# A state-space convolution beside a memory attention: one load moved to the head of the second half, and the projections dealt out in another way

## The chip, the cores and the metric

The kernel runs on one core of a Trainium2 chip. The time is device microseconds of one execution; of the kernel before there are three, 894.51, 900.52 and 901.75 us, median 900.52. A further execution was taken with the hardware profiler. Its trace gives every instruction of the engines: TensorE (PE, with its weight loads as PEld), VectorE (DVE), ScalarE (ACT), GpSimd (POOL) and SyncE (SP), which issues most of the DMAs.

## The reference, cut to what matters

The input is `u`, 2048 rows of 448 columns. Two branches are mixed by a gate: `g * a + (1 - g) * b`, with `g = sigmoid(sum(u * gate_w))`.

```
# a: a long convolution per channel d; its kernel K sums 256 decaying rotations
P = exp((A * dt)[:, :, None] * pos)            # [448, 256, 2048], complex
K = 2 * einsum("dn,dnl->dl", C, P).real
y = irfft(rfft(K, 4096) * rfft(u, 4096))[:2048] + u * D_skip
# b: 16 heads of 28, 4 segments of 512 rows, a running memory M, z
p = softmax(q k^T * scale + mask);  a_dot = p v
a_mem = (phi(q) M) / (phi(q) z + 1e-6)
o = sig(beta) * a_mem + (1 - sig(beta)) * a_dot
M += phi(k)^T v;  z += sum(phi(k));  out = o @ wo
```

All is float32. The projections `x @ wq`, `x @ wk`, `x @ wv` are done in split precision, as three products of high and low parts.

## The kernel before, in words

**First half** (`first_half`, line 310). It builds `K`. Channels are taken 16 at a time: `J` runs over 28 blocks, and each block has two passes `n = 2J, 2J+1` of 8 channels. Four passes make a group, numbered `g = n // 4`, from 0 to 13. One factor of a rotation is an exponential (`EY`, `EX`), the other a sine and a cosine (`cs`), and ACT needs another table for Exp than for Sin. So all six exponentials of a group (two blocks, three each, `blk` 0 to 2) are made together, by `decays(g)` (line 427), and the four passes follow. Each exponential takes its argument from a small matmul pair into a PSUM tile `arg`, of which there are two. In the kernel before, `exponents` (line 341) issues that pair and `decay` (line 348) the exponential, and the pair for the next slot is issued ahead of the exponential of this one. The first pair of a group is issued before `sums(n - 1)` of the pass before (line 463), and the eight matmuls of `turns(4 * g)`, the angles of the next pass, come in slot 5, ahead of its exponential (line 435). `turns` uses the same two `arg` tiles.

A pass `n` does, in the order of the program: `turns(n + 1)` on PE, `trig(n)` (three ACT instructions), some of the projections (`feed.spend`), `product(n)` (four DVE instructions into `X` and `Y`), `sums(n - 1)` (64 small matmuls). PE keeps the order of the program; in this half (`k.strict`) so do ACT and DVE.

**Feed** (class at line 472). The projections of the other branch and the first transform of `u` are written as a generator of small steps, each of which tells its cost in us. `spend(us)` adds credit (at most 4.0 in hand) and takes steps until the credit is used. It stops at a step of negative cost, whose result must first be read. It also stops at the mark "pe": two finished projections then hold two of the three PSUM tiles `m` until the next `decay` calls `feed.exps`, which issues their exponentials and copies on ACT (`e`, `hi`, four instructions) while the Exp table is loaded. While feed is held or done, a step of the transform of `u` (`ut`, `gs`) is taken instead. A pass gives 2.0 (line 458), a slot of `decays` 1.1 (line 441). With `k.exps` set (slots 2 to 5), copies of the feed go to DVE instead of ACT.

**Second half** (`second_half`, line 1256). It opens with `transform_k` (line 547), whose PSUM tiles are copied by ACT (line 567) and DVE and stored to `GK`; then 16 units of attention run (`maxima`, `weigh`, `values`), with the convolution (`convolve`, line 574) dealt between them. Here a planner with its own model of time orders the instructions of ACT, DVE, POOL and SP; PE keeps the order of the program. `load_wo` (line 984) is called after the second unit. It loads `wo` and three constants on SP's queue. One of them is the selecting matrix `c_sel` (32 x 512), which goes to a tile `selin` and is copied by ACT into `k.sel`; `spread` (line 1124) uses it to bring reciprocals of denominators to all rows, for the first time at 608 us. `selin` lies in the room of the tile `am`.

Of the kernel before, what the change touches and what calls it, by code (L numbers as in the profile page):

```python
# [12 lines left out]
F32 = mybir.dt.float32  # L13
# [3 lines left out]
AF = mybir.ActivationFunctionType  # L17
# [10 lines left out]
SEG = 512  # L28
# [281 lines left out]
def first_half(nc, k, gy, feed):  # L310
# [3 lines left out]
    NJ = 28  # L314
    act, v = k.act, nc.vector
    lt, EY, EX, kps, arg, cs, XY = {}, {}, {}, {}, {}, {}, {}
    exps = []

    def load_decay(J, queue=nc.sync.dma_start):
        lt[J] = k.lhs[J % 5]  # L320
# [12 lines left out]
    def load(J):  # L333
        if J < NJ:
            load_decay(J)
            load_phase(J)

    def rows(nt):
        return slice(64 * nt, 64 * nt + 64), {"tile_position": (64 * nt, 0)}

    def exponents(J, blk):

        exps.append(k.ps("arg"))
        for nt in range(2):
            r, kw = rows(nt)
            k.mm(exps[-1][:, nt], lt[J][r, 2], k.ce[r, blk], start=True, stop=True, **kw)

    def decay(J, blk):
        pt = exps.pop(0)
        if blk < 2:  # L350
            out = EY[J, blk] = gy.tile([128, 2, 512], F32, tag="EY", name="EY", bufs=6)
        else:
            out = EX[J] = gy.tile([128, 2, 512], F32, tag="EX", name="EX", bufs=2)
        feed.exps()
        act(out, pt, AF.Exp, scale=-1.0)
        if blk == 2 and J > 1:
            scale(J)

    def scale(J):
        o = EX[J]  # L360
        if True:
            cab = k.cab[:, :, 16 * J : 16 * J + 16].unsqueeze(3).broadcast_to([128, 2, 16, 32])
            o = o.rearrange("p t (d c) -> p t d c", c=32)
            nc.gpsimd.tensor_tensor(o, o, cab, ALU.mult)  # L364

    def turns(n):

        J, c = divmod(n, 2)
        arg[n] = pt = k.ps("arg")
        for nt in range(2):  # L370
            r, kw = rows(nt)
            k.mm(pt[:, nt], lt[J][r, c], k.ct[r, 0], start=True, stop=False, **kw)
        for i in range(2):
            for nt in range(2):
                r, kw = rows(nt)
                k.mm(pt[:, nt], k.one[r], k.mag[r, i : i + 1].broadcast_to([64, 512]), start=False, stop=False, **kw)
        for nt in range(2):
            r, kw = rows(nt)
            k.mm(pt[:, nt], lt[J][r, c], k.ct[r, 1], start=False, stop=True, **kw)

    def trig(n):

        pt = arg.pop(n)
        cs[n] = t = gw.tile([128, 2, 2, 2, 256], F32, tag="cs", name="cs", bufs=2)
        pv = pt.rearrange("p t (w c) -> p t w c", w=2)
        act(t[:, 1].rearrange("p w t c -> p t w c"), pv, AF.Sin, scale=TWO_PI)
        act(t[:, 0].rearrange("p w t c -> p t w c"), pv, AF.Abs)
        fl = t[:, 0].rearrange("p w t c -> p (w t c)")
        act(fl, fl, AF.Sin, bias=k.bhp, scale=-TWO_PI)

    def product(n):
        J, c = divmod(n, 2)
        t = cs.pop(n)
        X = gw.tile([128, 2, 2, 256], F32, tag="X", name="X", bufs=2)
        Y = gw.tile([128, 2, 16, 64], F32, tag="Y", name="Y", bufs=2)
        XY[n] = X, Y
        ex = EX[J][:, :, 256 * c : 256 * c + 256].unsqueeze(1).broadcast_to([128, 2, 2, 256])
        v.tensor_tensor(X, ex, t[:, :, 0], ALU.mult)  # L398
        ey = EY.pop((J, c)).rearrange("p t (d c) -> p (t d) c", c=64)
        y = t[:, :, 1].rearrange("p r t (d c) -> p r (t d) c", c=32)  # L400
        lo = ey[:, :, :32].unsqueeze(1).broadcast_to([128, 2, 16, 32])
        v.tensor_tensor(Y[:, :, :, :32], lo, y[:, :, :, ::-1], ALU.mult)  # L402
        v.tensor_tensor(Y[:, 0, :, 32:], ey[:, :, 32:], y[:, 0], ALU.mult)  # L403
        v.scalar_tensor_tensor(Y[:, 1, :, 32:], ey[:, :, 32:], -1.0, y[:, 1], ALU.mult, ALU.mult)  # L404

    def sums(n):
        g, h = divmod(n, 4)
        X, Y = XY.pop(n)
        if h == 0:
            kps[g] = k.ps("k")  # L410
        k.turn_over(kps[g][:, 2 * h : 2 * h + 2], 0)
        for q in range(2):
            for i, (nt, r) in enumerate(((0, 0), (0, 1), (1, 0), (1, 1))):
                for j in range(4):
                    d = 4 * q + j
                    k.mm(
                        kps[g][32 * j : 32 * j + 32, 2 * h + q],
                        X[:, r, nt, 32 * d : 32 * d + 32],
                        Y[:, r, 8 * nt + d],
                        start=(i == 0),  # L420
                        stop=(i == 3),
                        tile_position=(0, 32 * j),
                    )
        if h == 3:
            v.tensor_copy(k.kb[:, :, 8 * g : 8 * g + 8].rearrange("p b q -> p q b"), kps.pop(g))

    def decays(g):
        slots = [(J, blk) for J in (2 * g, 2 * g + 1) for blk in range(3)]
        if g == 0:
            exponents(*slots[0])  # L430
        for i, (J, blk) in enumerate(slots):
            if i < 5:
                exponents(*slots[i + 1])
            elif g > 0:
                turns(4 * g)
            decay(J, blk)
            if g > 0 and i == 4:
                sums(4 * g - 1)
            if g > 0:
                k.exps = i >= 2  # L440
                feed.spend(1.1)
                k.exps = False

    room = []
    yield load_decay, load_phase, functools.partial(decays, 0), room
    gw = room[0]
    scale(0)
    scale(1)
    turns(0)
    for n in range(2 * NJ):  # L450
        if n < 4:
            load(n + 2)
        elif n % 2 == 0:
            load(n // 2 + 4)
        if n % 4 < 3:
            turns(n + 1)
        trig(n)
        feed.spend(2.0)
        product(n)
        if n == 2 * NJ - 1:  # L460
            feed.fill(2)
        if n % 4 == 3 and n + 1 < 2 * NJ:
            exponents((n + 1) // 2, 0)
        if n % 4 > 0:
            sums(n - 1)
        if n % 4 == 3 and n + 1 < 2 * NJ:
            decays(n // 4 + 1)
    feed.fill(4)
    sums(2 * NJ - 1)

# [506 lines left out]
def attend(nc, k, ap):  # L977
# [2 lines left out]
    wo = ap.tile([128, 4, D], F32, name="wo")  # L980
    k.den = ap.tile([128, 128], F32, name="den")
    k.sel = ap.tile([32, 4, 128], F32R, name="sel")

    def load_wo():
        nc.gpsimd.memset(wo, 0.0)
        for j in range(4):
            k.ldma(
                wo[32 * j : 32 * j + 28], k.wo.rearrange("(g j e) c -> j e g c", j=4, e=28)[j]
            )
        k.ldma(k.den, k.c_den)  # L990
        t = ap.tile([128, 4, SEG], F32, tag="am", name="selin", bufs=1)[:32, 0]
        k.ldma(t, k.c_sel.rearrange("p g c -> p (g c)"))
        nc.scalar.activation(k.sel.rearrange("p g c -> p (g c)"), t, AF.Copy)
        k.ldma(k.dbc, k.D_skip.unsqueeze(0).broadcast_to([128, D]))

    Q, K, W, Vs, pvss = {}, {}, {}, {}, {}
# [130 lines left out]
    am = {}  # L1127
# [128 lines left out]
def second_half(nc, k, ap, tp, fp, fin, lp):  # L1256
# [7 lines left out]

    nothing = iter(())
    attend(nc, k, ap)
    k.load(0)
    k.load_rest(0)
# [116 lines left out]
def gated_mix(ctx, tc, k):  # L1385
# [168 lines left out]
    with ExitStack() as st:  # L1554
# [25 lines left out]
        with ExitStack() as s2:  # L1580
            early, prm = pool(s2, "early"), pool(s2, "prm", "right")
            feed = Feed(work(project(nc, k, pp, prm, tu)), tu)
            half = first_half(nc, k, gy, feed)
            load_decay, load_phase, decays, room = next(half)
            params = prepare_params(nc, k, prm, early, gp)
            n = next(params)
            k.ct = gp.tile([128, 2, 512], BF16, name="ct")
            constants()
            while n is not None:
                if n == "decays":  # L1590
                    for J in range(2):
                        load_decay(J, k.pdma)
                    nc.sync.dma_start(k.ct, k.c_ct)
                    decays()
                elif n == "phases":
                    load_phase(0)
                    k.held_by.append(load_phase(1).ins)
                else:
                    feed.until(feed.count + n)
                n = next(params, None)  # L1600
# [69 lines left out]
```

## Time and profile before

| what | value |
|---|---|
| three timed executions | 894.51, 900.52, 901.75 us |
| the profiled execution | 905.99 us, its span 904.2 us |
| mean clock granted to PE over the span | 0.91 |
| first half: the last `sums` end at | 454.8 us |
| Exp and Sin table loads from 115.89 us on | 24, two in each of 12 groups |
| load of `selin`: issue, copy on ACT | 540.00 us, 546.74 us |

A row of the timeline gives the start, the length, the engine, the line, the operation, and the tiles written and read; in square brackets stands how long the engine was idle before, and what ended that. Where a line is that of a helper (1395 for ACT, 1430 for PE), the tile's name tells the instruction. `ps_arg<-ce` are arguments of exponentials, `ps_arg<-ct` and `ps_arg<-mag` are `turns`, `ps_k` are `sums`, `ps_m` are the projections.

### The profile page before, as it was taken

The numbers are of one execution on the slowest core, as the hardware profiler recorded it, in microseconds if no ns is written. First come the engines' busy times: TensorE is split into PE (matmuls) and PEld (weight loads), VectorE is DVE, ScalarE is ACT, GpSimd is POOL, SyncE is SP. The second block draws the span as 40 slices with busy tenths as digits, with TensorE's granted clock in tenths as the row PEclk, the third lists the DMA queues.
The fourth block names the chain that finished last, engine by engine and source line by source line (L and its number), as shares of the span: only waits on it lengthen the run. The fifth ranks groups of instructions, "written<-read, shape, count | busy, mean of one in ns | idle before, by whom it ended". The sixth has DMA issues, their size and how long they took to land.

```text
span 904.2 us, 19002 instructions
## 1 busy us (share of the span) xinstructions
PE 767.8 (85%) x7508; PEld 413.7 (46%) x7517; DVE 600.0 (66%) x1158; ACT 537.1 (59%) x640; POOL 191.0 (21%) x273
## 2 busy tenths in 40 slices
PE   1676997899887999879787997999998999888997
PEld 1353654564454565446443443444444444334433
DVE  7985569766479757687857454556465656665564
ACT  4875689888789788888812344545354534342320
POOL 5222211011110011100100211232323232333210
PEclk9996999999898999989968597999999999888799
DMA  9258844223434324220377765678577575456773
GB/s 234 82 143 287 251 142 133 80 79 107 120 123 127 101 97 150 94 83 14 140 248 270 248 178 149 227 234 279 171 232 253 174 236 179 150 192 226 203 237 100
DMA packets 93408, 153.15 MB, mean 169 GB/s; under 512 B 21544, under 2 KB 58040, under 8 KB 93320
## 3 DMA queue, kind: packets, MB, share of 16 engines
q1 hardware_dynamic: 82104, 136.13, 47.6%
q10 hardware_dynamic: 8032, 10.26, 3.2%
q0 software_dynamic: 3184, 5.56, 2.3%
q8 instruction: 59, 0.97, 0.5%
q14 instruction: 29, 0.24, 0.1%
HBM read 90.91 MB, written 60.63 MB: 168 GB/s over the span
## 4 chain that ended last, share of the span: by engine, by line
PE 56%; DVE 16%; ACT 12%; DMA 8%; issue 5%; SPq 1%; POOL 1%; DVEq 0%; ACTq 0%; POOLq 0%
PE ps_m L1430 18%; PE ps_a L1430 18%; PE ps_pv L1430 8%; PE ps_arg L1430 6%; ACT cs L1395 5%; PE ps_k L1430 4%; DVE jk L1048 4%; DVE Y L402 3%; PE ps_m L1433 2%; DVE X L398 2%; DVE Y L403 1%; DMA RD<-rs 1%; DVE pr L611 1%; ACT hi L1395 1%; ACT L1395 1%
## 5 line engine op out<-in xcount | busy, mean ns | idle before, releaser
L1048 DVE CUSTOM_DVE_ANT_0 jk<-ps_a,mk 128x512 f32<-128x512 f32 (+3 forms) x256 | 125.0, 488 | 55.3 <-PE ps_a L1430 48.2
L1081 ACT ACTIVATE PT<-ps_a 128x1024 f32<-128x1024 f32 (+1 forms) x96 | 84.6, 882 | 119.4 <-PE ps_a L1430 110.1
L364 POOL TENSOR_TENSOR EX<-EX,cab 128x1024 f32<-128x1024 f32 x28 | 54.0, 1931 | 318.3 <-ACT EX L1395 274.2
L1395 ACT ACTIVATE cs<-ps_arg 128x1024 f32<-128x1024 f32 x111 | 107.3, 1020 | 9.7 <-PE ps_arg L1430 8.5
L1430 PE MATMUL ps_a<-qu,ku 32*128 32x512 f32 (+3 forms) x768 | 93.7, 366 | 8.5 <-ACT PT L1081 6.8
L1430 PE MATMUL ps_k<-Y,X 128*32 128x64 f32 x3584 | 67.2, 231 | 30.6 <-DVE Y L403 30.2
L1086 POOL TENSOR_SCALAR_AFFINE_SELECT PT<-PT 128x256 f32<-128x256 f32 x128 | 52.2, 421 | 182.6 <-ACT PT L1081 173.6
L398 DVE TENSOR_TENSOR X<-EX,cs 128x1024 f32<-128x1024 f32 x56 | 69.7, 1245 | 23.2 <-ACT cs L1395 23.1
L1430 PEld LDWEIGHTS ps_k<-Y,X 128*32 128x32 f32 x3584 | 57.5, 117 | 54.5 <-DVE Y L403 44.7
L1430 PE MATMUL ps_m<-xh,w 112*128 112x512 f32 x192 | 76.2, 440 | 1.7 <-ACT gs L1395 1.0
L1430 PEld LDWEIGHTS ps_a<-qu,ku 32*128 32x128 f32 x768 | 65.5, 203 | 16.9 <-ACT PT L1081 7.3
L402 DVE TENSOR_TENSOR Y<-EY,cs 128x1024 f32<-128x1024 f32 x56 | 70.0, 1250 | 0.0
L1430 PE MATMUL ps_arg<-ce,lh 64*128 64x512 bf16 x168 | 40.8, 443 | 30.6 <-ACT EY L1395 20.0
L1395 ACT ACTIVATE cs<-cs,bhp 128x1024 f32<-128x1024 f32 x56 | 64.4, 1151 | 1.8
L1430 PEld LDWEIGHTS <-lh 64*128 64x128 bf16 x392 | 22.5, 96 | 81.3 <-issue 69.1
L1395 ACT ACTIVATE EY<-ps_arg 128x1024 f32<-128x1024 f32 x52 | 52.1, 1040 | 9.2 <-PE ps_arg L1430 9.1
L1430 PE MATMUL ps_a<-ku,qu 32*128 32x512 f32 (+3 forms) x256 | 48.0, 415 | 9.8 <-DVE mx L1048 8.6
L1430 PEld LDWEIGHTS ps_a<-ku,qu 32*128 32x128 f32 x256 | 23.4, 199 | 57.6 <-issue 26.6
L1430 PEld LDWEIGHTS ps_m<-xh,w 112*128 112x128 f32 x192 | 38.1, 198 | 23.6 <-issue 9.4
L404 DVE SCALAR_TENSOR_TENSOR Y<-EY,cs 128x512 f32<-128x512 f32 x56 | 40.5, 725 | 11.7 <-ACT cs L1395 11.0
L1430 PE MATMUL ps_arg<-ct,lh 64*128 64x512 bf16 x224 | 45.3, 390 | 0.8 <-ACT cs L1395 0.8
L1430 PE MATMUL ps_pv<-PT,V 128*32 128x128 f32 (+3 forms) x512 | 45.0, 499 | 0.0
(229 smaller groups left out, 1462.0 us busy)
## 6 DMA issues: line engine op xcount, KB each, us to landing
w<-WD SPq DMA_DIRECT2D x24, 448.0 KB, 3.9
qu<-QD SPq DMA_DIRECT2D x32, 256.0 KB, 4.2
ku<-KD SPq DMA_DIRECT2D x32, 256.0 KB, 4.4
GU<-gs SPq DMA_DIRECT2D x32, 224.0 KB, 2.6
GK<-gs SPq DMA_DIRECT2D x8, 896.0 KB, 3.7
gk<-GK SPq DMA_DIRECT2D x32, 224.0 KB, 5.4
gu<-GU SPq DMA_DIRECT2D x32, 224.0 KB, 2.5
BB<-bs ACTq DMA_DIRECT2D x16, 448.0 KB, 4.8
```

The costliest lines, as they stand in the source:

```text
L364: nc.gpsimd.tensor_tensor(o, o, cab, ALU.mult)
L398: v.tensor_tensor(X, ex, t[:, :, 0], ALU.mult)
L402: v.tensor_tensor(Y[:, :, :, :32], lo, y[:, :, :, ::-1], ALU.mult)
L403: v.tensor_tensor(Y[:, 0, :, 32:], ey[:, :, 32:], y[:, 0], ALU.mult)
L404: v.scalar_tensor_tensor(Y[:, 1, :, 32:], ey[:, :, 32:], -1.0, y[:, 1], ALU.mult, ALU.mult)
L611: nc.vector.tensor_tensor(pr[c], pt, ks.pop(c), ALU.mult)
L1048: v.tensor_tensor_reduce(junk[:, :n], pt[:, x, o : o + n], k.mk[:, SEG - n :], 1.0, -3e38, ALU.add, ALU.max, mx[:, 3 - t, h : h + 1],)
L1081: nc.scalar.activation(PT[b, hp], pt[:, :, :n], AF.Exp, scale=SCALE)
L1086: nc.gpsimd.affine_select(sl, sl, [[0, 2], [1, 128]], ALU.is_ge, 0.0, base=0, channel_multiplier=-1)
L1395: x = op(*args, **kw)
L1430: tc.keep_in_program_order(nc.tensor.matmul(*args, **kw))
L1433: tc.keep_in_program_order(nc.tensor.transpose(*args))
```

## The change

It has three parts. `exponents` goes, and `decay` makes its argument in its own slot, right before its exponential; the first pair of a group no longer goes ahead of `sums`, and `turns(4 * g)` is issued after the last slot. The credit of a pass becomes 2.8 and that of a slot 1.4. The load of `c_sel` goes from `load_wo`, on SP's queue, to the head of the second half, on POOL's, with its copy on ACT behind it.

```diff
-    def exponents(J, blk):
-
-        exps.append(k.ps("arg"))
+    def decay(J, blk):
+
+        pt = k.ps("arg")
         for nt in range(2):
             r, kw = rows(nt)
-            k.mm(exps[-1][:, nt], lt[J][r, 2], k.ce[r, blk], start=True, stop=True, **kw)
-
-    def decay(J, blk):
-        pt = exps.pop(0)
+            k.mm(pt[:, nt], lt[J][r, 2], k.ce[r, blk], start=True, stop=True, **kw)
...
     def decays(g):
-        slots = [(J, blk) for J in (2 * g, 2 * g + 1) for blk in range(3)]
-        if g == 0:
-            exponents(*slots[0])
-        for i, (J, blk) in enumerate(slots):
-            if i < 5:
-                exponents(*slots[i + 1])
-            elif g > 0:
-                turns(4 * g)
-            decay(J, blk)
-            if g > 0 and i == 4:
-                sums(4 * g - 1)
-            if g > 0:
-                k.exps = i >= 2
-                feed.spend(1.1)
-                k.exps = False
+        for J in (2 * g, 2 * g + 1):
+            for blk in range(3):
+                decay(J, blk)
+                if g > 0 and J % 2 and blk == 1:
+                    sums(4 * g - 1)
+                if g > 0:
+                    k.exps = 3 * (J % 2) + blk >= 2
+                    feed.spend(1.4)
+                    k.exps = False
...
-        feed.spend(2.0)
+        feed.spend(2.8)
         product(n)
         if n == 2 * NJ - 1:
             feed.fill(2)
-        if n % 4 == 3 and n + 1 < 2 * NJ:
-            exponents((n + 1) // 2, 0)
         if n % 4 > 0:
             sums(n - 1)
         if n % 4 == 3 and n + 1 < 2 * NJ:
             decays(n // 4 + 1)
+            turns(n + 1)
...
     k.sel = ap.tile([32, 4, 128], F32R, name="sel")
+    selin = ap.tile([128, 4, SEG], F32, tag="am", name="selin", bufs=1)[:32, 0]
+    k.pdma(selin, k.c_sel.rearrange("p g c -> p (g c)"))
+    nc.scalar.activation(k.sel.rearrange("p g c -> p (g c)"), selin, AF.Copy)
 
     def load_wo():
...
         k.ldma(k.den, k.c_den)
-        t = ap.tile([128, 4, SEG], F32, tag="am", name="selin", bufs=1)[:32, 0]
-        k.ldma(t, k.c_sel.rearrange("p g c -> p (g c)"))
-        nc.scalar.activation(k.sel.rearrange("p g c -> p (g c)"), t, AF.Copy)
```

More of the change, by code (lines that the diff above doesn't have):

```diff
@@ L316, in first_half @@
     lt, EY, EX, kps, arg, cs, XY = {}, {}, {}, {}, {}, {}, {}
-    exps = []
     def load_decay(J, queue=nc.sync.dma_start):
```

## The prediction

> **What bounds the kernel now.** I read the page first, for the shares and the chain that ended last.
>
> ```profile
> span 904.2 us, 19002 instructions
> PE 767.8 (85%) x7508; PEld 413.7 (46%) x7517; DVE 600.0 (66%) x1158; ACT 537.1 (59%) x640; POOL 191.0 (21%) x273
> PE 56%; DVE 16%; ACT 12%; DMA 8%; issue 5%; SPq 1%; POOL 1%; DVEq 0%; ACTq 0%; POOLq 0%
> ```
>
> The chain is mostly TensorE, but the change touches the first half (to 455 us) and one load of the second, so each is read by itself. ScalarE changes its table twice in each group of the first half: at the head of `decays` (Exp) and at the head of the four passes behind it (Sin). Those 24 loads cut it into stretches. Here are rows of the view of engine busy time by stretch, first for the decays of groups 2 to 13 (columns: stretch, its length, busy time of PE, PEld, DVE, ACT, POOL, then PE's granted clock), then for the passes.
>
> ```profile
> 144.51:155.10 10.59, 7.53 (x140) 4.63 (x144) 10.16 (x16) 10.05 (x13) 1.91 (x1) 0.84 0.56 167
> 283.02:294.50 11.48, 8.42 (x138) 5.34 (x142) 10.66 (x17) 10.12 (x14) 1.91 (x1) 0.72 0.60 181
> 396.58:407.91 11.33, 8.37 (x150) 5.07 (x142) 10.53 (x16) 10.12 (x14) 1.91 (x1) 0.70 0.34 125
> sum 138.84, PE 116.46 PEld 72.22 DVE 89.08 ACT 111.89 POOL 22.99; mean PE 9.70 PEld 6.02 DVE 7.42 ACT 9.32 POOL 1.92
> ```
>
> ```profile
> 183.82:202.09 18.27, 18.23 (x284) 12.33 (x280) 13.04 (x18) 14.41 (x16) 1.92 (x1) 0.95 0.15 51
> 294.50:313.71 19.21, 18.71 (x298) 11.30 (x290) 14.52 (x19) 14.41 (x16) 1.91 (x1) 0.99 0.33 102
> 326.41:341.33 14.92, 14.92 (x199) 9.95 (x195) 11.84 (x15) 14.42 (x15) 1.92 (x1) 1.00 0.24 81
> 407.91:425.49 17.58, 17.57 (x256) 11.88 (x248) 14.79 (x21) 14.95 (x16) 1.91 (x1) 1.00 0.05 17
> 434.20:449.80 15.60, 12.01 (x235) 7.15 (x232) 13.37 (x17) 14.73 (x17) 2.44 (x2) 0.89 0.34 115
> sum 195.07, PE 171.26 PEld 103.71 DVE 157.41 ACT 174.99 POOL 23.51; mean PE 14.27 PEld 8.64 DVE 13.12 ACT 14.58 POOL 1.96
> ```
>
> In decays ACT is busy 9.32 of 11.57 us on average: ACT sets their length, and PE waits, at a lowered clock. In four passes PE is busy 95% or more and sets the length (the first four rows: mean 17.5). The other eight, of which the last row is one, share (195.07 - 69.98) / 8 = 15.6 us each, whatever projections they carry: ACT and DVE set those. Projections dealt into such a pass are free, up to a point.
>
> Why PE waits in decays is shown by the waits of PE (115.89 to 449.8 us) and the timeline of ACT and PE in group 12.
>
> ```profile
> PE ps_arg L1430 <- ACT EY L1395: 13.7, 7, 2.9
> PE ps_arg L1430 <- ACT EX L1395: 5.3, 6, 1.5
> 396.58 1.28 ACT L1395 ACT_TABLE_LOAD   x1
> 397.87 0.60 ACT L1395 ACTIVATE e<-ps_m 128x512 f32<-128x512 f32 x1
> 399.89 1.05 ACT L1395 ACTIVATE EY<-ps_arg 128x1024 f32<-128x1024 f32 x1
> 396.34 1.10 PE L1430 MATMUL ps_k<-Y,X 128*32 128x64 f32 x64 [1.41 <-DVE Y L403]
> 397.37 0.39 PE L1430 MATMUL ps_arg<-ce,lh 64*128 64x512 bf16 x2
> 397.69 0.65 PE L1433 MATMUL ps_m<-ident,xin 128*112 128x128 f32 x4
> 400.99 0.61 PE L1430 MATMUL ps_arg<-ce,lh 64*128 64x512 bf16 x2 [2.64 <-ACT EY L1395]
> ```
>
> A held pair of projections puts four readings of PSUM ahead of the first exponential (from 397.87 to 399.89). PE, an argument ahead, finds both banks full and stands 2.64 us. Such waits sum to 19.0 us.
>
> **The change part by part.**
>
> *Dealing.* I followed the credits of `feed` step by step, before and after, and priced the steps by the timeline of PE, start to start: from 413.73 to 416.46 there are twelve projection matmuls, so six take 1.36, and three of the slightly longer ones (512 columns for 450) 0.78. The others are 0.91 (`ut`), 1.06 (`macc`, up to the `turns` at 409.15), 0.58 (`ph`), 1.09 (`pkT`, up to the `turns` at 412.76) and 0.65 above (`xin`).
>
> ```profile
> 436.34 0.91 PE L1430 MATMUL ps_m<-ut,s1u 64*128 64x448 f32 x2
> 408.09 1.12 PE L1430 MATMUL ps_m<-ph,macc 128*128 128x512 f32 x2
> 410.12 0.66 PE L1433 MATMUL ps_m<-ident,ph 128*128 128x128 f32 x4
> 410.70 0.39 PE L1430 MATMUL ps_arg<-ct,lh 64*128 64x512 bf16 x2
> 411.67 1.16 PE L1430 MATMUL ps_m<-v,pkT 128*128 128x128 f32 x8
> 413.73 0.47 PE L1430 MATMUL ps_m<-wvh,xh 112*128 112x450 f32 x1
> ...
> 416.46 1.10 PE L1430 MATMUL ps_k<-Y,X 128*32 128x64 f32 x64
> ```
>
> Either way the same 172 us are dealt. Passes of groups 1 to 13 carry, in us: before 9.4, 4.1, 7.4, 7.0, 3.6, 3.5, 3.5, 9.2, 8.0, 6.3, 4.4, 9.3, 3.6; after 11.1, 3.5, 8.8, 10.0, 5.2, 3.8, 9.2, 10.0, 5.2, 3.8, 9.3, 2.7, 0. Decays: before 10.5, 7.9, 4.1, 7.9, 7.4, 7.3, 7.3, 4.2, 6.8, 7.5, 7.5, 4.2, 6.4; after 11.3, 7.9, 4.3, 8.2, 7.3, 7.9, 4.2, 8.2, 7.3, 7.9, 4.2, 7.3, 0. So after, everything is spent in pass 50 of 0 to 55. The last group's 10.0 us, free today (its pass is a 15.6), move forward.
>
> The four PE-set passes carry 7.0, 9.2, 8.0, 9.3: mean 8.4, which leaves 9.1 of their 17.5 as the rest. After, five carry 8.8 or more (47.3 together): 5 x 9.1 + 47.3 = 92.8. Seven light ones at 15.6 make 109.4. Sum 202.2 against 195.07: **+7.1**. Group 1 gets 2.5 more, under loads of weights that hold it anyway: between 0 and +2.5, I take +1, since its feed is the largest of all.
>
> *Arguments in their own slot.* PE no longer runs an argument ahead; ACT's exponential waits for its own matmuls, and queued behind it on ACT are the other exponentials, the table load and the sines that DVE needs. Decays are then PE's: 0.8 us from the table load to the first argument (396.58 to 397.37), six arguments at 0.32 (397.37 to 397.69), one `sums` at 1.03 (396.34 to 397.37), the projections of slots 0 to 4, and one exponential, 1.02: 4.8 + projections. Slot 5 holds 1.09, 1.09, 1.36, 1.56, 0.58, 0.58, 1.36, 1.56, 0.58, 0.58, 0.91 in groups 2 to 12, so slots 0 to 4 hold 74.7 - 11.3 = 63.4 in these eleven, and 11 x 4.8 + 63.4 = 116.2. Three groups (3, 7, 11) begin with transposes that need banks the held pair frees late; today's three such (10.59, 11.48, 11.33) average 11.1 against 8.3 by the formula: +8.4. The last group, without projections, is ACT's, some 7.7. Sum 132.3 against 138.84: **-6.5** at full clock. Of it PE has 63.4 + 11 x 2.95 (arguments and `sums`) = 96 us on the path, and the twelve decays ran at a mean clock of 0.89 (the three shown and nine of 0.75 to 1.00). Between 0.89 (96 / 0.89 - 96 = +11.9, so +5.4 in all) and 1 (-6.5) I take 0.945 (+5.6), since the 19 us of waits that lowered it partly go: **-0.9**.
>
> *`turns(4g)` behind the last slot.* It takes 0.97 (410.70 to 411.67). It is done slot 5's feed + 0.97 after the last argument; ACT needs 1.02 + 1.28 for exponential and table load. Only a slot of over 1.33 makes ACT wait, by 0.23 at most: nothing in the sum, hidden by the table load; at half clock it would be about 1.8 a group.
>
> *The selecting matrix.* Today its load stands behind `wo`, and its copy on ACT ahead of exponentials PE waits for. Timeline, SP's and ACT's queues and PE:
>
> ```profile
> 535.34 3.40 SPq L1446 DMA_DIRECT2D wo<-in_B_wo  x4
> 540.00 0.33 SPq L1446 DMA_DIRECT2D selin<-in_c_sel  x1
> 542.22 0.41 ACTq L625 DMA_DIRECT2D BB<-bs  x1
> 546.74 0.63 ACT L993 ACTIVATE sel<-selin 32x512 fp32r<-32x512 f32 x1 [9.34 <-DMA selin<-in_c_sel]
> 547.28 1.00 ACT L1081 ACTIVATE PT<-ps_a 128x1024 f32<-128x1024 f32 x1
> 548.33 1.01 PE L1430 MATMUL ps_a<-qu,ku 32*128 32x384 f32 x4 [6.80 <-ACT PT L1081]
> ```
>
> Without it, next late is ACT's own issue of `BB`, done at 542.63: the exponential moves from 547.28 to 542.63. Gain between that 4.65 and the whole 9.34; I take **-4.7**, the nearer row, as the loads of `wo` that delay `BB` stay. SP loses one issue of 0.33 there. Added at the head: an issue on POOL, a transfer, a copy of 0.63 on ACT.
>
> ```profile
> 454.84 1.59 POOL L985 MEMSET wo<- 128x1792 f32 x1 [6.10 <-PE ps_k L1430]
> 459.39 0.92 ACT L567 ACTIVATE gs<-ps_a 128x896 f32<-128x896 f32 x1 [9.19 <-PE ps_a L1430]
> qu<-mn POOLq DMA_DIRECT2D x32, 8.0 KB, 3.5
> ```
>
> Room comes free at about 454.84. With the 3.5 us of POOL's small loads it lands at some 458.9 with its issue, in the 9.19 us that ACT stands idle: 0. With the 6.7 that it took from 540.00 to 546.74, it lands at 462.1, and the first `gs`, if queued behind the copy, starts 3.3 us late with PE's banks behind it. I take 0. POOL's own next work can wait (its next DMA starts 30 us later).
>
> [...]
>
> *Sum:* +7.1 + 1 - 0.9 - 4.7 = **+2.5** on the profiled execution (905.99, its span 904.2 and 1.8 around it), so 908.5. That execution lies 5.5 above the median of 900.52, to which a prediction is compared; on the median it is **903.0**.
>
> **The rivals.**
>
> 1. *PE's clock sets the decays* (slower). Place: decays, where PE now is on the path with 96 us. Point: 96 x (1/c - 1) = 6.5, a clock c of 0.94; below, decays get longer than today's. For it: today's rows of 0.70 to 0.84. Against: half of the waits behind them go. At 0.85 it is +16.9 - 6.5 = +10.4, and 7.1 + 1 + 10.4 - 4.7 = +13.8: **914**. [...]
> 2. *Waits go, the stall goes whole* (faster). Clock 1 in decays, the 9.34 all gained, and PE's half-clock work behind the stall (0.50 and 0.57 below, 6.7 us busy) back at full: another -3. +7.1 + 1 - 6.5 - 9.3 - 3 = -10.7: **890**. Against: `BB` stays late.
>
> ```profile
> 545.00:550.00 5.00, 1.68 (x12) 1.67 (x12) 0.74 (x2) 3.26 (x5) 0.89 (x2) 0.50 0.37 138
> 550.00:555.00 5.00, 5.00 (x12) 2.09 (x10) 2.67 (x9) 1.65 (x3) 1.40 (x4) 0.57 0.40 121
> ```
>
> 3. *The stall only moves* (the change doesn't do what it says). The copy waits at the head instead, in front of `gs`, for the late landing: 2.5 + 3.3 = +5.8, **906**. For it: SP's loads start at the same moment as POOL's. Against: 9.19 us of idle ACT.
>
> **How the numbers follow.** Chances: forecast 0.45, rival 1 0.30, rival 2 0.13, rival 3 0.12. The range, 888 to 917, takes in all four centres and leaves out the far side of rival 1 and of rival 2. A measurement tells about 1% (9 us) from no change. Faster by that, under 891.5: most of rival 2 and a little of the forecast's low end, 0.13. Slower, over 909.5: three quarters of rival 1, the bad end of the forecast and of rival 3, 0.34. Between: 0.53.
>
> **What would show it.** Decays' lengths between table loads near 11 us with PE busy nearly throughout, ACT waiting for `ps_arg`, PE's 19 us on EY and EX mostly gone; five passes of 17.5 to 19; a last group without projections, hardly shorter than 15.6; ACT on PT at some 5 us after `bs` near the load of `wo`. I am wrong if heavy passes cost more than 19, if decays lengthen by over 1 us each, if the second half is reordered by the new place of `selin`, or if the stall's gain is eaten by a later wait.

## The result, and the profile after

The changed kernel took 911.37 us (median; 904.44 to 921.80) against 903.24 us of the kernel before in the same runs (894.51 to 914.28). The ratio is 1.0119, with a 95% interval of 1.0091 to 1.0146: **slower by 1.2%, some 10.7 us**. A second measurement, among the experiments below, gave 1.0112 (1.0069 to 1.0155). The forecast was +2.5 us (903.0). The ratios leave out executions that count as slow and the medians are over all, so that the two can differ by some 3 us: the medians lie 8.1 us apart here.

The page of the changed kernel gives the shares and the chain that ended last (the helpers' lines are 1384 for ACT and 1419 for PE in this kernel):

```profile
span 902.7 us, 19026 instructions
PE 753.9 (84%) x7517; PEld 411.1 (46%) x7517; DVE 599.9 (66%) x1159; ACT 537.8 (60%) x639; POOL 191.7 (21%) x274
PE 51%; DVE 16%; ACT 14%; DMA 12%; issue 5%; POOL 1%; SPq 1%; DVEq 0%; ACTq 0%; POOLq 0%
```

This one execution (904.44 us) is the fastest of those behind its median, and that of the kernel before (905.99) lies above its own. The two pages alone would show a gain. So stages are compared here, and verdicts come from the ratios.

PE is on the chain for less (51% against 56%), DMA for more (12% against 8%), but the chain doesn't say where. The stages do: the first half ends 9.9 us later (464.6 for 454.8), and 7.2 of that are group 1's. These are the engines' busy times by stretch (length; PE, PEld, DVE, ACT, POOL; granted clock, DMA share, GB/s), cut at the Exp load that begins group 1, at the matmul that waits for its weights, and at the Exp load that begins group 2. First the kernel before, then the changed one:

```profile
80.33:101.06 20.73, 14.64 (x108) 8.38 (x108) 7.30 (x9) 11.05 (x13) 7.33 (x5) 0.68 0.98 312
101.06:115.89 14.83, 14.83 (x191) 9.85 (x192) 11.82 (x14) 12.59 (x14) 0.00 (x0) 1.00 0.67 207
```

```profile
81.11:101.90 20.79, 10.85 (x104) 6.66 (x101) 7.21 (x9) 10.29 (x12) 7.33 (x5) 0.91 0.98 311
101.90:123.86 21.96, 21.48 (x258) 14.11 (x262) 14.35 (x17) 13.68 (x16) 0.00 (x0) 0.91 0.53 168
```

Group 1 took 35.56 us before and takes 42.75: **+7.2**. Up to the arrival of the weights both are alike in length (20.73 and 20.79) with the DMA engines at 98%, and in all eleven profiles of this document in which PE waits there it is 20.1 to 22.2 us: what PE does meanwhile hardly moves it. Behind it PE was busy without a gap for 14.83 us; now it is busy for 21.48. What it can do before the weights come is therefore free, and what is left for afterwards is paid.

Ahead of the weights both kernels do the same 24 projection matmuls and the same `sums`. The changed kernel lacks the eight matmuls of `turns(4)` there; its busy time is shorter (10.85 us against 14.64) mainly because its clock is higher (0.91 against 0.68). Behind the weights it does more: nine projection matmuls (2.0 us, at 1.36 for six), two of `ut` (0.91), the eight of `turns` (0.97) and 48 of `sums` (0.8, at 1.03 for 64). Another 1.9 us go to half clock, which lasts until 105.7 (0.50 over these 3.80 us). That is 6.6 of the 6.65 us. The timeline shows what stands behind the weights:

```profile
101.90 0.77 PE L1419 MATMUL ps_m<-xh,w 112*128 112x512 f32 x1 [6.74 <-DMA w<-WD]
106.98 1.02 ACT L1384 ACTIVATE cs<-ps_arg 128x1024 f32<-128x1024 f32 x1 [9.43 <-PE ps_arg L1419]
```

The last slot of the decays takes a projection whose weights are still on the way (at the old rates too, as the experiment on the own slot shows). PE stands 6.74 us, and `turns(4)`, now queued behind it, keeps ACT's sines waiting for 9.43. In the kernel before `turns(4)` went ahead of that projection, and ACT hardly waited for the angles. PE, at half clock until 93.5 (0.50 from 80.33 on), came to the projection later, and waited little for the same weights:

```profile
100.42 1.94 ACT L1395 ACTIVATE cs<-ps_arg 128x1024 f32<-128x1024 f32 x2 [0.54 <-PE ps_arg L1430]
101.06 0.47 PE L1430 MATMUL ps_m<-xh,w 112*128 112x512 f32 x1 [0.69 <-DMA w<-WD]
```

Now the decays and the passes of groups 2 to 13 (same columns), some rows of each and the sum:

```profile
123.86:135.67 11.81, 10.80 (x139) 6.88 (x128) 5.93 (x10) 9.34 (x12) 1.92 (x1) 1.00 0.69 220
268.11:280.51 12.40, 9.00 (x104) 4.73 (x104) 11.94 (x18) 10.23 (x14) 1.92 (x1) 0.86 0.58 182
354.12:368.07 13.95, 13.49 (x172) 8.03 (x162) 8.24 (x13) 9.49 (x12) 1.92 (x1) 0.88 0.26 95
sum 143.48, PE 121.75 PEld 75.34 DVE 99.28 ACT 113.07 POOL 23.00; mean PE 10.15 PEld 6.28 DVE 8.27 ACT 9.42 POOL 1.92
```

```profile
163.67:182.30 18.63, 16.00 (x253) 10.56 (x255) 14.12 (x18) 14.45 (x15) 1.91 (x1) 1.00 0.13 37
194.57:211.04 16.47, 16.47 (x252) 10.75 (x254) 13.03 (x17) 14.58 (x16) 1.91 (x1) 1.00 0.39 126
338.79:354.12 15.33, 11.72 (x200) 6.53 (x202) 11.17 (x15) 14.81 (x16) 1.91 (x1) 1.00 0.33 94
sum 192.92, PE 154.63 PEld 96.67 DVE 147.29 ACT 175.16 POOL 24.03; mean PE 12.89 PEld 8.06 DVE 12.27 ACT 14.60 POOL 2.00
```

Decays went from 138.84 to 143.48 (+4.6), passes from 195.07 to 192.92 (-2.1). In the decays PE is busy 121.75 us (116.46 before) and stands still 21.7 (22.4 before). The waits of PE over these groups (us in total, times, longest) show an exchange:

```profile
PE ps_k L1419 <- DVE Y L399: 31.2, 20, 3.2
PE ps_arg L1419 <- ACT cs L1384: 7.5, 8, 2.2
PE ps_m L1422 <- DVE lo L757: 7.0, 2, 3.6
PE ps_arg L1419 <- ACT EY L1384: 4.1, 6, 1.5
PE ps_m L1419 <- ACT pkT L1384: 3.7, 4, 1.2
PE ps_m L1422 <- DVE lo L759: 3.1, 1, 3.1
```

The wait on `EY` fell from 13.7 to 4.1, as the own slot promised, and others that sum to 21.3 us (`cs`, `lo`, `pkT`; 1.5 before) stand in its place. The longest, on `Y`, was 24.9 over the same groups.

In the second half the selecting matrix and the place where it used to stall are these lines of the timeline:

```profile
456.63 0.54 POOL L973 DMA_DIRECT2D selin<-in_c_sel  x1 [9.27 <-DVE Y L399]
459.85 0.63 ACT L974 ACTIVATE sel<-selin 32x512 fp32r<-32x512 f32 x1
469.18 0.92 ACT L556 ACTIVATE gs<-ps_a 128x896 f32<-128x896 f32 x1 [8.70 <-PE ps_a L1419]
546.40 0.41 ACTq L614 DMA_DIRECT2D BB<-bs  x1
546.86 1.02 ACT L1070 ACTIVATE PT<-ps_a 128x1024 f32<-128x1024 f32 x1 [3.94 <-PE ps_a L1419]
547.94 1.07 PE L1419 MATMUL ps_a<-qu,ku 32*128 32x384 f32 x12 [0.89 <-ACT PT L1070]
```

The copy waits for nothing (no bracket) and is done before the last `sums` end; ACT's first `gs` follows their end by 4.5 us (4.6 before). `BB` is as late as the forecast had it, but PE's wait for `PT` fell from 6.80 us to 0.89.

### The profile page after: what moved, and what is told of

Same layout as the page of the kernel before. It is cut to its first block, busy times and chain, and to the rows that moved or that the text cites. A ratio compares the mean times of both kernels' runs of the same rounds, so it can differ in the third digit from the quotient of the medians.

```text
span 902.7 us, 19026 instructions
## 1 busy us (share of the span) xinstructions
PE 753.9 (84%) x7517; PEld 411.1 (46%) x7517; DVE 599.9 (66%) x1159; ACT 537.8 (60%) x639; POOL 191.7 (21%) x274
## 4 chain that ended last, share of the span: by engine, by line
PE 51%; DVE 16%; ACT 14%; DMA 12%; issue 5%; POOL 1%; SPq 1%; DVEq 0%; ACTq 0%; POOLq 0%
PE ps_m L1419 18%; PE ps_a L1419 15%; PE ps_pv L1419 7%; ACT cs L1384 6%; PE ps_arg L1419 5%; PE ps_k L1419 4%; DVE jk L1037 3%; DVE Y L398 2%; DMA dn<-pvs 2%; PE ps_m L1422 2%; DMA RD<-rs 2%; DVE X L394 1%; ACT L1384 1%; DMA WD<-wsp 1%; DVE Y L399 1%
## 5 line engine op out<-in xcount | busy, mean ns | idle before, releaser
L1419 PE MATMUL ps_a<-qu,ku 32*128 32x512 f32 (+3 forms) x768 | 90.5, 357 | 2.3 <-DVE mx L1037 0.9
L394 DVE TENSOR_TENSOR X<-EX,cs 128x1024 f32<-128x1024 f32 x56 | 69.7, 1245 | 22.9 <-ACT cs L1384 22.3
L1419 PE MATMUL ps_m<-xh,w 112*128 112x512 f32 x192 | 72.8, 431 | 7.8 <-DMA w<-WD 6.7
L1419 PEld LDWEIGHTS ps_a<-qu,ku 32*128 32x128 f32 x768 | 63.1, 197 | 11.1 <-issue 3.7
L1419 PE MATMUL ps_arg<-ct,lh 64*128 64x512 bf16 x224 | 42.9, 392 | 8.6 <-ACT cs L1384 8.1
L1419 PE MATMUL ps_arg<-ce,lh 64*128 64x512 bf16 x168 | 37.5, 426 | 12.1 <-ACT EY L1384 6.9
L1419 PE MATMUL ps_m<-wo,pvs 128*128 128x448 f32 x96 | 42.7, 591 | 3.4 <-ACT tb L1167 1.4
```

Source lines behind the costliest of these rows:

```text
L1419: tc.keep_in_program_order(nc.tensor.matmul(*args, **kw))
```

## The experiments

The ratios are against the kernel before in the same runs; 0.01 is some 9 us.

| kernel | median us, before | ratio (95%) |
|---|---|---|
| early selecting matrix only | 896.80, 902.38 | 0.9960 (0.9916 to 1.0003) |
| arguments in own slot only | 903.93, 902.38 | 1.0003 (0.9964 to 1.0042) |
| dealing 2.8 and 1.4 only | 920.01, 899.72 | 1.0224 (1.0174 to 1.0273) |
| dealing 2.8 and 1.4 in group 1 only | 908.83, 901.02 | 1.0124 (1.0081 to 1.0168) |
| changed, selecting matrix behind `wo` | 919.61, 902.38 | 1.0188 (1.0134 to 1.0242) |
| changed, again | 909.27, 899.72 | 1.0112 (1.0069 to 1.0155) |
| changed, `turns` ahead of last dealing | 907.41, 902.38 | 1.0034 (0.9992 to 1.0075) |
| changed, old rates in group 1 | 901.44, 899.72 | 1.0028 (0.9992 to 1.0064) |
| changed, both of these | 901.30, 902.08 | 1.0015 (0.9980 to 1.0051) |
| changed, eight more matmuls at the head | 912.02, 901.02 | 1.0126 (1.0073 to 1.0179) |
| before, early matrix, 1.4 and 0.8 in group 1 | 895.67, 901.02 | 0.9957 (0.9921 to 0.9992) |

And the stages of each profiled execution in us, read from the timeline: group 1 (Exp load to Exp load), groups 2 to 13 (to the end of the last `sums`), the head (to ACT's first reading of `ps_pv`), the stretch with the load of `wo` (to the second reading), and the fourteen readings behind it:

| kernel | group 1 | 2 to 13 | head | `wo` | rest |
|---|---|---|---|---|---|
| before | 35.6 | 338.9 | 64.7 | 28.7 | 339.8 |
| before, second profile | 35.6 | 337.8 | 64.6 | 29.0 | 342.5 |
| early matrix only | 35.5 | 335.9 | 61.4 | 22.4 | 338.3 |
| own slot only | 39.4 | 340.9 | 55.9 | 28.4 | 338.9 |
| dealing only | 39.6 | 353.3 | 55.9 | 27.6 | 343.6 |
| dealing in group 1 only | 42.5 | 341.7 | 55.7 | 28.4 | 335.8 |
| changed, matrix behind `wo` | 43.0 | 344.9 | 61.4 | 27.9 | 340.1 |
| changed | 42.8 | 340.8 | 60.7 | 22.4 | 339.1 |
| changed, again | 42.7 | 344.2 | 60.8 | 21.6 | 339.3 |
| changed, `turns` ahead | 43.0 | 342.8 | 60.9 | 22.3 | 338.6 |
| changed, old rates in group 1 | 40.2 | 344.4 | 55.6 | 21.8 | 339.2 |
| changed, both | 38.3 | 342.8 | 59.6 | 21.8 | 338.0 |
| changed, more matmuls | 44.4 | 341.4 | 64.0 | 22.5 | 339.0 |
| before, early matrix, less in group 1 | 33.1 | 342.7 | 65.4 | 21.5 | 339.5 |

Each row is one execution, so a stage is uncertain by some 3 us (compare the two of the same kernel). The head lies between 55.6 and 65.4, whatever the edit.

**Early selecting matrix only.**

```diff
     k.sel = ap.tile([32, 4, 128], F32R, name="sel")
+    selin = ap.tile([128, 4, SEG], F32, tag="am", name="selin", bufs=1)[:32, 0]
+    k.pdma(selin, k.c_sel.rearrange("p g c -> p (g c)"))
+    nc.scalar.activation(k.sel.rearrange("p g c -> p (g c)"), selin, AF.Copy)
...
-        t = ap.tile([128, 4, SEG], F32, tag="am", name="selin", bufs=1)[:32, 0]
-        k.ldma(t, k.c_sel.rearrange("p g c -> p (g c)"))
-        nc.scalar.activation(k.sel.rearrange("p g c -> p (g c)"), t, AF.Copy)
```

> Kernel before with the selecting matrix loaded at the head of the second half, nothing else. Theory A (the change's loss of 10.7 us is made in the first half, where the traces show +9.9, and the earlier load is a gain of its own): the exponential PT near the loads of wo comes some 6 us earlier, and the time is 4 to 6 us under the kernel before. Theory B (the second half gives nothing back in an ordinary execution; the 6 us in one profile are eaten later): PT comes earlier in the profile, but the time is within 2 us of the kernel before.

Measured: 0.9960, 3.6 us by the ratio and 5.6 by the medians, the interval just touching 1. Theory A is the nearer one. Its timeline shows what became of PE's stall of 6.80 us:

```profile
538.60 1.12 PE L1430 MATMUL ps_a<-qu,ku 32*128 32x384 f32 x12 [0.95 <-ACT PT L1081]
```

In the table the stretch of `wo` is 27.6 to 29.0 us wherever the matrix is loaded behind `wo` and 21.5 to 22.5 wherever it is loaded early, in every kernel: 6.3 us on the means.

**The changed kernel without that move.** The three lines go back behind the load of `den`.

> Changed kernel with the selecting matrix loaded behind wo as before: arguments in their own slot, dealing at 2.8 and 1.4. Theory A: +10.7 and the 5 us that the earlier load gained, so some +15 us against the kernel before. Theory B: +10 to +11, as with the earlier load. In both the first half ends some 10 us later than in the kernel before (464 to 465 us).

Measured: 1.0188, +17 us. Beside 1.0112 and 1.0119 of the changed kernel the early load is worth 6 to 7 us here as well. Theory A again; the second half does give its gain, and the loss is all in the first half.

**Own slot only.** The changed kernel with the selecting matrix behind `wo`, and the old rates:

```diff
-                    feed.spend(1.4)
+                    feed.spend(1.1)
...
-        feed.spend(2.8)
+        feed.spend(2.0)
```

> Arguments in their own slot and turns(4g) behind the last slot, with the old dealing of 2.0 and 1.1 and the old place of the selecting matrix. Theory A (the place of arguments and turns makes the loss): group 1 still longer than 35.6 us, decays of groups 2 to 13 longer than 138.8 by 4 us or more, the time +8 to +12 us. Theory C (the dealing makes the loss): within 3 us of the kernel before, group 1 at 35.6.

Measured: 1.0003. Theory A, which was ours after the two traces, fell: on balance the place of the arguments and of `turns` costs nothing by itself. Its profile has group 1 longer by 3.8 us, with a wait for the weights that is nearly the changed kernel's, and a head shorter by nearly 9:

```profile
102.01 0.77 PE L1419 MATMUL ps_m<-xh,w 112*128 112x512 f32 x1 [6.29 <-DMA w<-WD]
```

ACT's sines wait 8.65 us behind it. The first half ends at 461.2, 6.4 us later than in the kernel before, and in this execution the head makes up for it. So that wait alone doesn't decide the time.

**Dealing only.** The kernel before with `feed.spend(2.8)` in the passes and `feed.spend(1.4)` in the decays.

> Kernel before with the dealing at 2.8 and 1.4 alone (arguments a slot ahead, turns ahead of the last slot, selecting matrix behind wo). Theory D (the dealing costs by itself): passes of groups 2 to 12 longer than 179.5 us by 6 to 10, group 1 by 2 to 4, time +8 to +14 us. Theory E (dealing costs only together with the arguments in their own slot, where PE has no argument in hand): time within +-3 us of the kernel before. By the prediction's terms, +8.

Measured: 1.0224, **+20 us**, twice the whole change. Theory D, and more than it expected. Here the order of before is kept, so passes can be compared with the prediction's price; the stretches of two heavy ones (groups 4 and 5):

```profile
192.36:211.40 19.04, 19.04 (x240) 12.37 (x243) 14.09 (x18) 14.57 (x16) 1.92 (x1) 1.00 0.35 110
222.25:241.83 19.58, 17.60 (x256) 10.71 (x252) 12.62 (x16) 14.92 (x17) 1.91 (x1) 0.87 0.26 81
```

The passes with 10.0 us of projections take 19.04: nearly the 9.1 + feed of the prediction, and its five heavy ones take 93.6 together (forecast 92.8). But the one with 5.2 takes 19.58 (the other such one 19.86), which the prediction had put among the light ones at 15.6, with PE busy 17.60 at a clock of 0.87.

**Dealing in group 1 only.**

```diff
-                feed.spend(1.1)
+                feed.spend(1.4 if g == 1 else 1.1)
...
-        feed.spend(2.0)
+        feed.spend(2.8 if n < 8 else 2.0)
```

> Kernel before with 2.8 and 1.4 a slot in group 1 alone (2.0 and 1.1 behind it). Theory F (what is dealt into group 1 beyond the old rates is paid in full, since PE is busy without a gap from the arrival of its late weights): group 1 at 38 to 40 us instead of 35.6, and the time 2 to 5 us over the kernel before, although later passes get less. Theory G (the price is the same wherever it is dealt): within 1.5 us of the kernel before.

Measured: 1.0124, +11 us (8 by the medians): this edit alone costs as much as the whole change, and about half of the dealing. Theory F, at about twice its price. Group 1 takes 42.5 us. Its timeline shows the weights later (104.50 for 101.06; PE stands 2.00 for 0.69) and a thing that was not foreseen: the dealing now gets through its projections and begins on the next sort of work, whose reading `gs` ACT must do ahead of its table load (the changed kernel has it as well, at 123.29, after a wait of 2.82).

```profile
104.50 0.47 PE L1430 MATMUL ps_m<-xh,w 112*128 112x512 f32 x1 [2.00 <-DMA w<-WD]
124.22 0.55 ACT L1395 ACTIVATE gs<-ps_m 128x448 f32<-128x448 f32 x1 [3.34 <-PE ps_m L1430]
124.78 1.28 ACT L1395 ACT_TABLE_LOAD   x1
```

**The changed kernel, old rates in group 1.** The mirror of it: `feed.spend(1.1 if g == 1 else 1.4)` and `feed.spend(2.0 if n < 8 else 2.8)`.

> The changed kernel with 2.0 and 1.1 a slot in group 1 only, 2.8 and 1.4 behind it. Theory F (a good part of the loss sits in group 1, where everything behind the late weights is PE's): group 1 at 39 to 40 us instead of 43, and the time 3 us or more under the changed kernel's. Theory G (what isn't dealt there is paid in later passes at the same price): group 1 shorter by as much, later passes longer, the time within 1.5 us of the changed kernel's.

Measured: 1.0028 against 1.0112, so 7 to 8 us come back. By the time theory F holds. The profile agrees only in part: group 1 falls to 40.2, but the first half ends at 467.8, no earlier than in the changed kernel (464.6 and 468.0), and what this execution gains, 5 us, is in its head (55.6 against 60.8).

**The changed kernel, `turns` ahead.**

```diff
                 if g > 0:
+                    if J % 2 and blk == 2:
+                        turns(4 * g)
                     k.exps = 3 * (J % 2) + blk >= 2
                     feed.spend(1.4)
...
             decays(n // 4 + 1)
-            turns(n + 1)
```

> Changed kernel with one edit: turns(4g) is issued ahead of the last slot's dealing instead of behind it. Theory A: the sines of group 1 no longer wait 9.43 us for a load of weights; group 1 falls from 42.8 to about 36 us, and the time from +10.7 to about +3 us against the kernel before. Theory C (the dealing itself, or waits that it only moves): the 7 us come back in group 1's passes or in the next decays, and the time stays at +9 to +11 us.

Measured: 1.0034, 7 us under the changed kernel by the ratios (3 to 5 by the medians), as theory A expected of the time. But its reason is not seen: group 1 is as long as before the edit. The timeline has the sines at 98.22 in place of 106.98, and PE's wait for the weights as long as ever:

```profile
98.22 1.94 ACT L1385 ACTIVATE cs<-ps_arg 128x1024 f32<-128x1024 f32 x2
103.26 0.77 PE L1420 MATMUL ps_m<-xh,w 112*128 112x512 f32 x1 [6.57 <-DMA w<-WD]
```

This execution (906.27) is no faster than those of the changed kernel, so where the other runs gain isn't shown.

**Both together.**

> The changed kernel with both edits that helped it: turns(4g) ahead of the last slot's dealing, and 2.0 and 1.1 a slot in group 1. Each alone brought the ratio from 1.012 to about 1.003. Theory R (both mend the same loss, PE's late weights in group 1): no further gain, ratio 0.999 to 1.006. Theory S (they mend different losses, the one of turns in all groups): the gains add, ratio 0.992 to 0.997.

Measured: 1.0015. Theory R: the two gains do not add. That both mend one loss, PE's work behind the late weights of group 1, fits the profile, in which group 1 is 38.3; but with `turns` ahead alone group 1 stayed at 43.0, so for that edit it is not shown.

**The changed kernel again, and the kernel before again.**

> The changed kernel once more, for a second profile beside the same runs of the kernel before. If the first half's loss is the change's own, the last sums end 10 to 16 us later than 454.8 again (464.7 in the first profile, 470.8 with the same first half and the selecting matrix behind wo). If the lag in the first profile was the chance of one execution, it falls under 5 us. Time +9 to +12 us against the kernel before.

> The kernel before once more, for a second profile. Expected by every theory: first half ends at 453 to 457 us; from there to the first reading of ps_pv 60 to 65 us (64.7 in the first profile, 61.4 with the selecting matrix early); 28 to 29 us to the second reading, with PE idle some 6 us ahead of the exponential PT.

Measured: the last `sums` end at 468.0 in the changed kernel and at 453.5 in the kernel before, so the lag of the first half is the change's own. The rest came as expected for both.

**Less in group 1.** The early matrix, and `feed.spend(0.8 if g == 1 else 1.1)` and `feed.spend(1.4 if n < 8 else 2.0)` in the kernel before.

> Kernel before with the selecting matrix loaded at the head and only 1.4 and 0.8 a slot in group 1, so that some 5 us of projections go from group 1 to later groups, the last one among them. Theory F: group 1 falls under 33 us, the time is 8 to 11 us under the kernel before (5 to 6 of it the load's). Theory G: the load's 5 to 6 us alone, and longer passes behind group 1.

Measured: 0.9957 (0.9921 to 0.9992), a version that is faster than both kernels, but no faster than the early matrix alone (0.9960). Theory G: group 1 is shorter by 2.5 us (33.1), groups 2 to 13 longer by more (342.7). What is paid above the old rates is not to be had back below them.

**More matmuls at the head.** Eight matmuls behind the last `sums`, into a bank that nobody reads, because the head's length seemed to go with the moment at which it begins.

```diff
     sums(2 * NJ - 1)
+    pad = k.ps("arg")
+    for i in range(4):
+        for nt in range(2):
+            r, kw = rows(nt)
+            k.mm(pad[:, nt], lt[NJ - 1][r, 2], k.ce[r, 0], start=True, stop=True, **kw)
```

> The changed kernel with eight more matmuls of 64 by 512 behind the first half's last sums, written to a bank that nobody reads (0.9 us of PE at full clock, 1.7 at half). In ten profiles the time from the last sums to the first reading of ps_pv is 55.6 to 55.9 us where the last sums end 1.9 to 2.4 us after a tick of the grid of 3.41 us on which PE's granted clock changes, 60.7 to 61.4 where it is 0.3 to 0.5, and 61 to 65 where it is 2.8 to 3.0. Theory P (that phase sets the time): from 0.4 the pad moves it to 1.3 to 2.2, the stretch falls to about 56 us, and the time by 3 to 4 us against the changed kernel. Theory Q (the phase doesn't set it): the stretch stays at 60.8 and the time grows by 0 to 2 us.

Measured: 1.0126, and a head of 64.0 us, although the eight end at 467.8, 2.3 us behind the tick at 465.5. Theory P fell. The time is 1 to 3 us over the changed kernel, near theory Q, though the stretch grew rather than stay.

## Why the prediction was right and wrong

The sign and the range held; the size did not: +2.5 us forecast, some +10.7 measured, which is nearer to rival 1's 914. That the range held says little: it reaches from a gain of 12 us to a loss of 16.

- **Group 1, "between 0 and +2.5, I take +1": this step failed.** The profile has +7.2, and the dealing of group 1 alone costs 8 to 11 us of time. The loads of weights hold the group, as the prediction said, but that covers only what PE does *ahead* of their arrival. From there on PE was already busy 14.83 of 14.83 us, and that row stood in the trace of before. What was dealt more, 2.5 us by the prediction, cost 2.9 there. The rest is what came with it: `turns` and 48 matmuls of `sums` that now lie behind the arrival (1.8) and a stretch at half clock (1.9, with 0.77 us for a matmul that takes 0.47). The two edits to group 1's dealing alone (+8 to +11 us and -8 us) show where the cost is set; how much of it is paid in group 1 itself is less sure, as the profile of the second has its gain in the head.
- **`turns(4g)` behind the last slot, "nothing": wrong in group 1.** The step counted the projections of slot 5 by their duration, and did not ask whether they could start. Behind a wait of 6.74 us the covering table load of 1.28 is gone. Put back, 3 to 7 us of time return, and hardly more when the group's dealing is lowered too (ratio 1.0015 for both); where they return isn't shown. Under the old rates the same place cost nothing (1.0003), though ACT's sines waited 8.65 us there too.
- **Dealing +7.1 in the passes, decays -0.9: the split was wrong, and the sum came near because the two errors cancel, which is luck.** Groups 2 to 13 took 335.9 to 338.9 us in the three profiles that have the first half of before, and 340.8 to 344.9 in the five with the changed order and rates in all groups: +5.3 on the means, +6.2 forecast. In the profiles compared above it is only +2.5: passes fell by 2.1 and decays grew by 4.6. The price of 9.1 + feed holds where the order is that of before (19.04 for a feed of 10.0). In the changed kernel the same feed takes 16.47, so 6.5 + feed (the other three heavy passes, with 8.8 to 9.3, take 16.5 to 18.6). With the dealing only, PE does the projections of the last two slots behind the Sin load; in the changed kernel they stand ahead of it: in group 4, 38 matmuls of the feed lie behind that load, and 49 with the dealing only. The prediction put these projections into the decays (slot 5's beside the last exponential) and left them in the 9.1 as well. In the decays it let PE work nearly throughout; the waits on `EY` and `EX` went (19.0 to 5.4), but new ones came, and PE stands still for as long as before (21.7 us). In the other direction it missed that one-slot dealings of 5.2 make a pass heavy too (19.58), which shows only in the order of before.
- **The clock in decays, 0.945: right.** The twelve rows of the decays run at 0.86 to 1.00, mean 0.946. That fewer waits make it so, the prediction's reason, isn't shown: PE stands still in them 21.7 us in all, and 22.4 before. Rival 1's 0.85 throughout, which gave its 914, did not come; the time near 914 has another cause.
- **The selecting matrix, -4.7: right, and 1.6 too small.** 6.3 us in the stretch of `wo`. `BB`'s late issue is as forecast, but PE, once the copy is gone, has other work until then and waits only 0.89. The copy delays no `gs` (4.5 us behind the last `sums`, 4.6 before), and the load landed 2.1 us after its issue on POOL's queue (6.7 on SP's before): rival 3 is out. Rival 2 needed decays without waits and is out as well.

The stages do not close: group 1 (+7.2), groups 2 to 13 (+5.3) and the load (-6.3) make +6.2, and the times +8 to +11. The profiles of before lie 3 to 8 us above its medians (905.99 and 907.57 against 899.72 to 903.24), most of the others' near or under theirs. The one stage that varies by as much is the head, where the profiles of before have 64.7 and 64.6 (one other with a head of 65.4, that of less in group 1, is 5 us above its median too, at 900.66). That its other runs have a shorter head would close the account. The clocks on record point that way: the two profiled executions were granted 0.910 and 0.911 on average, and of 86 others of this kernel the median is 0.918; the 36 with 0.92 or more took 898.8 us on average, the 10 below 0.905 took 907.8. But no profile shows the head of such an execution, and it stays open.

## What to carry to other kernels

Ask of a stretch under a late load not whether it is covered, but which work lies ahead of the arrival and which behind: here the stretch ahead of it took 20.73 and 20.79 us with PE busy 14.64 and 10.85 of them, so that a us there was free; behind it PE was busy 14.83 of 14.83 us, and what came on top was paid (21.96); and `turns`, moved behind the first user of the load, waited with it, and ACT 9.43 us for `turns`. When work is moved across the mark by which stretches were measured, take it out of the one before adding it to the other. Measure the parts of a bundled change alone: here one part gained 4 to 6 us, one was neutral, and one cost 20, and the sum of the three isn't the time of the whole.

## What the runs showed of the hardware

The head, the stretch from the last `sums` to the first reading of `ps_pv`, took 55.6 to 65.4 us with nearly the same work in it. What differs is how long PE's clock is at half: the mean clock over the head is 0.84 where it takes 55.9 us, 0.77 at 59.7, 0.73 at 61.4 and 0.66 at 64.7 and 65.4, while PE stands still for 7 to 9 us in each. Stretches of the head of the kernel before, of the changed kernel, and of the changed kernel with old rates in group 1:

```profile
454.80:496.20 41.40, 34.89 (x186) 16.36 (x187) 26.32 (x76) 9.21 (x10) 3.33 (x4) 0.75 0.77 272
496.20:520.10 23.90, 22.62 (x124) 11.26 (x121) 10.89 (x41) 9.31 (x11) 5.10 (x12) 0.50 0.77 254
```

```profile
464.70:505.10 40.40, 33.51 (x179) 15.43 (x179) 25.83 (x75) 9.21 (x10) 3.29 (x4) 0.75 0.77 271
505.10:518.70 13.60, 13.42 (x71) 7.81 (x71) 7.71 (x29) 5.20 (x6) 3.87 (x9) 0.50 0.93 312
```

```profile
467.80:503.00 35.20, 28.37 (x177) 12.43 (x177) 25.77 (x75) 9.21 (x10) 3.28 (x4) 0.94 0.87 312
503.00:516.50 13.50, 13.14 (x67) 7.79 (x67) 7.71 (x29) 5.19 (x6) 3.83 (x9) 0.50 0.98 314
```

In the first two the clock also falls to half in the middle of the first stretch (mean 0.75), in the third it does not (0.94), and 5 us are the difference. The second stretch is at half clock all through, for 23.90 or 13.60 us, with PE busy 95% and 99% of it.

Read in steps of half a us, the clock stands at 0.50 or 1.00 but for the steps in which it changes, and the changes keep to a grid of 3.41 us: in the kernel before at 442.0, 445.5, 452.0, 462.5, 469.0, 483.0, 496.5 and 520.5, that is 1, 2, 3, 2, 4, 4 and 7 steps apart (78.5 us for 23 steps). In its second profile the changes (450.5, 461.0, 467.5, 481.5, 495.0, 519.0) are as far apart, and all 1.5 us earlier: in these two the grid's phase isn't tied to the start of the execution. Being busy did not bring the full clock back at the next step: for seven steps in a row (496.5 to 520.5) it stayed at half, with PE busy 22.62 of the 23.90 us from 496.20 to 520.10. What does bring it back isn't shown. That the phase at which the head begins sets its length, as the profiles had suggested, did not hold when eight matmuls moved it (a head of 64.0 us for 60.7 and 60.8); what does set it is open.
